# A grouped 1x1 convolution on one core: a longer head, unrolled pairs moved ahead of the loop, other store sizes at both ends, another relief for DMA engines

## The chip, the cores and the metric

One core of one Trainium2 chip runs the kernel. The metric is the device time in microseconds (us), median of several runs; before the change it was 478.7 us (three runs, 478.02 to 479.0). The record marks all executions told of here as fast; where one execution of a kernel took longer than another, it is called long, not slow. "PE" is the matmul engine, "ACT" the scalar engine, "DVE" the vector engine, "POOL" and "SP" two engines that here mostly issue transfers. The page counts 16 DMA engines for the core; they move the data between HBM and the on-chip memory, SBUF (here 201.57 MB in 10674 packets).

## The reference, cut to what matters

```python
def reference(x, w):              # x: 1 x 512 x 512 x 192, bf16;  w: 1 x 1 x 4 x 48 x 48
    ...
    # k = 1: each pixel's 4 groups of 48 channels are multiplied by 4 small matrices
    out = out + jnp.einsum('bhwgc,gcd->bhwgd', xg[:, i:i+H, j:j+W, :, :], w[i, j])
    return out.reshape(B, H, W, C)
```

262144 pixels of 192 bf16 channels are read and as many written: 100.7 MB each way. There is little arithmetic per byte.

## The kernel before

Each of the 128 partitions (rows) of SBUF takes a run of pixels; a "column" is one pixel per row, 384 bytes of it. Loads fill a ring of 240 columns, stores leave from a second ring of 280. Four columns are a "group", eight a "pair". For a pair, PE transposes 12 blocks and multiplies 12 blocks, DVE copies the transposed data, ACT copies ("casts") the result into the store ring. SP issues loads, ACT stores.

Two things are unusual. First, most of PE's program is a loop of 30 pairs, run 8 times, with unrolled pairs ahead of it and after it. Second, twice in the kernel 48 columns are moved as "120-row pieces": 8 of the 128 rows get no data there, and the rest is cut into blocks. In the trace one DMA engine gets no packet of these pieces (engine 4 below, idle for 1.9 us). In one of the two pieces some further rows move fewer columns (`UNEVEN`, "the relief").

```python
BIG = 80
SLOTS = 3
RCOLS = SLOTS * BIG                 # load ring, columns
OGRID = (72, 140, 212, 280)         # where stores end in the store ring
HEAD = (8, 24, 48)                  # first loads, columns
LATE_COLS = 240                     # the last 240 columns are stored in parts of 40,
LATE_PART = 40                      # the very last in 24, 20, 16 and 8
LAST_PARTS = (24, 20, 16, 8)
FULL = (("sync", 0, 128, 128, 0),)  # queue, first row, rows, outer size, columns less
PARTIAL = (
    ("sync", 0, 16, 4, 0), ("sync", 32, 16, 4, 0),
    ("pool", 52, 44, 11, 0), ("pool", 20, 12, 3, 0), ("pool", 96, 32, 8, 0),
)
UNEVEN = (("sync", 0, 16, 4, 16), *PARTIAL[1:])
FRONT = ((6, ((48, PARTIAL), (32, FULL))), (11, ((48, UNEVEN), (32, FULL))))
# ... (planning of fields, pieces, stores and of the loop cut)

            # PE
            for first, body, rounds in LOOPS:           # before: [(9, 30, 8)]
                for pair in range(pair, first):
                    step(pair)                          # unrolled: 9 pairs
                with pe.Fori(0, rounds):
                    for pair in range(first, first + body):
                        step(pair)
                pair = first + rounds * body
            for pair in range(pair, NP):
                step(pair)                              # unrolled: 8 pairs
# ...
            # ACT
            for g in range(NG):
                act.wait_ge(mm_done, g + 1)
                while todo and stores[todo[0]].g1 <= g - 1:
                    issue(todo.pop(0))                  # a store, when its last group is cast
                if over[g] is not None:
                    landed(over[g])                     # wait: the store last held in these columns
                v = 2 * g
                act.copy(out_columns(g).rearrange("p (u c) -> p u c", u=2),
                         o_ps[:, v % NOB:v % NOB + 2, 0:UC]).then_inc(...)
```

Of the kernel before, what the change touches and what calls it, by code (L numbers as in the profile page):

```python
# [1 line left out]

# [22 lines left out]
BIG = 80  # L25
SLOTS = 3
RCOLS = SLOTS * BIG
OGRID = (72, 140, 212, 280)
OCOLS = OGRID[-1]
HEAD = (8, 24, 48)  # L30
LATE_COLS = 240
LATE_PART = 40
LAST_PARTS = (24, 20, 16, 8)
NXP = 4
NXS = 3
NOB = 4
# [4 lines left out]
PARTIAL = (  # L41
    ("sync", 0, 16, 4, 0), ("sync", 32, 16, 4, 0),
    ("pool", 52, 44, 11, 0), ("pool", 20, 12, 3, 0), ("pool", 96, 32, 8, 0),
)
UNEVEN = (("sync", 0, 16, 4, 16), *PARTIAL[1:])
FRONT = ((6, ((48, PARTIAL), (32, FULL))), (11, ((48, UNEVEN), (32, FULL))))

FILL_ROWS = 5
FILL_BEFORE = (2, 3)


class Field:


    def __init__(self, cols, blocks, g0, pix):
        self.cols, self.g0, self.g1 = cols, g0, g0 + cols // 4
        self.full = blocks is FULL
        self.blocks = []
        for (queue, r0, rows, outer, less) in blocks:
            self.blocks.append((queue, r0, rows, outer, pix, cols - less))  # L60
            pix += rows * (cols - less)
        self.pix_end = pix
        assert cols % 4 == 0


class Piece:

    def __init__(self, i, field, c0, size):
        self.i, self.field = i, field
        self.c0, self.c1, self.size = c0, c0 + size, size  # L70
        self.g0, self.g1 = field.g0 + self.c0 // 4, field.g0 + self.c1 // 4
        self.at = 4 * self.g0 % RCOLS
        self.full, self.blocks = field.full, field.blocks
        assert size % 4 == 0 and self.at + size <= RCOLS

# [8 lines left out]
def plan_fields(npix):  # L84

    parts, head = [], sum(HEAD)
    for slots, special in FRONT:
        parts += [(head + BIG * slots, FULL), *special]
        head = 0
    cols = npix - sum((n - b[4]) * b[2] for n, blocks in parts for b in blocks)  # L90
    if cols < 128 * BIG:
        parts, cols = [], npix
    assert cols % 512 == 0
    fields, g, pix = [], 0, 0
    for n, blocks in [*parts, (cols // 128, FULL)]:
        fields.append(Field(n, blocks, g, pix))
        g, pix = fields[-1].g1, fields[-1].pix_end
    assert pix == npix
    return fields


def plan_pieces(fields):
    pieces = []
    for f in fields:
        first = [f.cols]
        if f.full:
            first = list(HEAD) if not f.g0 and sum(HEAD) <= f.cols else []
        c = 0
        while c < f.cols:
            n = first.pop(0) if first else min(BIG, f.cols - c)  # L110
            pieces.append(Piece(len(pieces), f, c, n))
            c += n
    return pieces


def plan_stores(fields):
    total = 4 * fields[-1].g1
    stores, at = [], 0
    for f in fields:
        c = 0  # L120
        if not f.full and at + f.cols > OCOLS:
            at = 0
        ends = []
        if f is fields[-1] and f.cols > LATE_COLS:
            ends = [f.cols - sum(LAST_PARTS[i:]) for i in range(len(LAST_PARTS))]
        while c < f.cols:
            if f.full:
                end = min([g for g in OGRID if g > at + 24] or [OCOLS]) - at + c
                if f.cols < BIG:
                    end = min(OCOLS - at + c, f.cols)  # L130
                if ends and c >= f.cols - LATE_COLS:
                    end = min(OCOLS - at, LATE_PART) + c
                end = min([end, f.cols] + [e for e in ends if e > c])
            else:
                end = f.cols
            stores.append(Store(f, c, end, at))
            c, at = end, (at + end - c) % OCOLS
    return stores


class Unit:


    def __init__(self, pieces):
        self.pieces, self.g0, self.g1 = pieces, pieces[0].g0, pieces[-1].g1
        self.slot = pieces[0].at // BIG
        self.regular = pieces[0].at % BIG == 0 and 4 * (self.g1 - self.g0) == BIG


def plan_units(pieces):  # L150
    units, rest = [], list(pieces)
    while rest:
        n = 1
        if rest[0].g0 and rest[0].at % BIG == 0:
            while n < len(rest) and rest[n].at % BIG:
                n += 1
        units.append(Unit(rest[:n]))
        rest = rest[n:]
    return units
# [19 lines left out]
def bass_standalone__grouped__vision_kernel(nc, x, w, out):  # L179
# [5 lines left out]
    fields = plan_fields(npix)  # L185
    pieces = plan_pieces(fields)
    stores = plan_stores(fields)
    units = plan_units(pieces)
    unit_of = {g: u for u in units for g in range(u.g0, u.g1)}
    store_of = {g: s for s in stores for g in range(s.g0, s.g1)}  # L190
# [12 lines left out]
    def transfers(ap, tile, part, queues):  # L203
        f, c0, c1, at = part.field, part.c0, part.c1, part.at
        for n, (queue, r0, rows, outer, pix, cols) in enumerate(f.blocks):
            if queue not in queues:
                continue
            px = ap[pix:pix + rows * cols, :]
            if f.full:
                view = px.rearrange("(p i) n -> p (i n)", p=rows)[:, c0 * C:c1 * C]  # L210
            else:
                assert (c0, c1) == (0, f.cols)
                view = px.rearrange("(c a i) n -> a c (i n)", a=outer, c=rows // outer)
            yield n, view, tile[r0:r0 + rows, at * C:(at + (c1 - c0 if f.full else cols)) * C]
# [12 lines left out]
    with ExitStack() as es:  # L227
# [25 lines left out]
        fill_sem = [sem(f"fill{k}") for k in range(4 * len(mixed))]  # L253

        def columns(g):
            at = 4 * g % RCOLS
            return ring[:, at * C:(at + 4) * C]

        def out_columns(g):
# [9 lines left out]
        def _(gp):  # L269
# [12 lines left out]
            def filler():  # L282
                k = len(used)
                src = xf[0:2 * FILL_ROWS, 0:4].rearrange("(t p) n -> p t n", t=2)
                dst = fill[:, 8 * k:8 * k + 8].rearrange("p (t n) -> p t n", t=2)
                gp.dma_start(dst, src).then_inc(fill_sem[k], 16)  # L286
                used.append(k)

            for nth, u in enumerate(mixed):
                part = [p for p in u.pieces if not p.full]  # L290
                for p in part:
                    gp.wait_ge(t_done, freed(p))
                    for n, dram, sbuf in transfers(xf, ring, p, ("pool",)):
                        if n in FILL_BEFORE:
                            filler()
# [6 lines left out]
                for i, s in enumerate(stores):  # L302
                    if any(s.field is p.field for p in part):
                        for n, dram, sbuf in transfers(of, oring, s, ("pool",)):
                            if n in FILL_BEFORE:
                                filler()
# [16 lines left out]
        def _(pe):  # L323
# [12 lines left out]
            def transposes(pair):  # L336
                todo = []
                for g in groups(pair):
                    u = unit_of[g]
                    if g % 2 and pair:  # L340
                        pe.wait_ge(e_done[(pair - 1) % NTOK], 1)
                    if g == u.g0:
                        for key in unit_keys[u]:
                            pe.wait_ge(ld_sem[key], 16)
                        todo += unit_keys[u] if u.regular else []
                    xg = columns(g)
                    for ul in range(2):
                        for tc in range(3):
                            j = ul * 3 + tc
                            last = pe.transpose(xT_ps[:, g % NXP, j * 128:(j + 1) * 128],  # L350
                                                xg[:, j * 128:(j + 1) * 128], ident[:])
                            if todo and 0 < j < 5:
                                last.then_inc(ld_sem[todo.pop(0)], -16)
                assert not todo
                last.then_inc(t_done, 1)
# [125 lines left out]
```

## Time and profile before

| what | value | where it stands |
|---|---|---|
| time | 478.7 us (three runs) | times |
| bytes moved, mean rate | 201.6 MB, 423 GB/s | page, DMA line |
| PE, ACT busy | 431.7, 388.3 us of 476.1 | page, part 1 |
| last cast ends | 467.7 us | timeline |
| last store lands | 475.6 us | landing times in the trace |

The page of the kernel before: PE's busy time and share, and of the 40 slices of the span the busy tenths of PE and DMA, and the GB/s in each slice:

```profile
PE 431.7 (91%) x6178; PEld 389.5 (82%) x6178; DVE 246.8 (52%) x258; ACT 388.3 (82%) x515; POOL 12.5 (3%) x28
...
PE   5999999999598999999998896999978979999991
...
DMA  8999999999999999999999999999999999999996
GB/s 330 439 394 431 429 423 432 432 430 428 435 431 429 434 421 435 435 429 433 439 431 428 428 436 433 424 427 434 433 434 424 439 422 425 433 432 432 420 424 287
```

DMA is at nine tenths or more in all slices but the first and the last, PE has dips. This reads as transfers that set the pace and compute that waits for them. The chain of waits says the same: its longest links (start, length, what) are four transfers.

```profile
89.78 39.13 DMA ring<-in_x_dram
...
239.06 49.44 DMA out_dram<-oring
...
306.59 44.66 DMA out_dram<-oring
...
385.64 44.65 DMA out_dram<-oring
```

The waits view (who waits for whom: total us, times, longest) shows what this costs ACT and PE:

```profile
ACT oring L446 <- DMA out_dram<-oring: 15.2, 7, 3.4
PEld xT_ps L350 <- POOLq L300: 5.1, 1, 5.1
```

The second line is the wait for a load of a 120-row piece (POOL collects its blocks). Then the windows view, two early stretches and the last two (window, length, busy us and count of PE, PEld, DVE, ACT and POOL, granted clock, DMA share, GB/s; a packet is counted whole in the window where it starts, so a share can pass 1):

```profile
12.00:24.00 12.00, 11.88 (x177) 10.72 (x175) 7.35 (x8) 10.90 (x15) 0.00 (x0) 1.00 1.04 448
24.00:36.00 12.00, 11.71 (x179) 10.75 (x177) 6.85 (x8) 10.87 (x15) 0.00 (x0) 1.00 0.96 380
...
456.00:468.00 12.00, 9.93 (x138) 8.44 (x136) 4.84 (x6) 10.45 (x14) 0.00 (x0) 1.00 0.99 413
468.00:480.00 12.00, 0.00 (x0) 0.00 (x0) 0.00 (x0) 0.00 (x0) 0.00 (x0) 0.61 0.38 155
```

The rate falls to 380 GB/s at 24 to 36 us although the engines are busy 0.96 of it. At the end, compute is over (no engine busy after 468 us) while DMA still works. The last line of the timeline (start, length) puts the last store's issue at 467.76 us, some 8 us ahead of its landing:

```profile
466.93 0.80 ACT L446 CAST oring<-o_ps 128x768 bf16<-128x768 f32 x1 [0.21 <-issue]
467.76 0.34 ACTq L427 DMA_DIRECT2D out_dram<-oring  x1
```

**Reading the packets one by one.** A DMA record in the trace has a start, a duration, a size and a queue, but no engine. It can be rebuilt: on a busy engine the next packet's record starts 4 ns before the last one's ends. Followed back from the 16 last packets, with each engine's order of sizes known from the plan, the records from 40 us on fall into 16 rows; 99.6% of 9593 steps have that 4 ns to within 6 ns. An engine's share of the 120-row pieces then tells its group. The kernel cuts these pieces into two blocks of 16 rows (SP loads and ACT stores them) and blocks of 44, 12 and 32 rows that POOL issues. (It also issues tiny filler transfers of 5 rows ahead of the 44-row and the 12-row block.) Of the 16 rebuilt rows four have packets of the SP and ACT blocks, one has none of the pieces, and eleven have POOL blocks, three of them from the 12-row block and eight from the 32-row block. They are called engines 0 to 3 (SP and ACT blocks), 4 (no block), 5 to 7 (12-row block) and 8 to 15 (32-row block) here. The numbers are names of groups: no record gives an engine's number.

When each engine's last packet ends, kernel before (us):

```
engines 0-3    470.3 470.5 472.8 473.4
engine  4      470.3                       (idle 1.9 us; no other group over 0.3 us)
engines 5-7    472.0 472.6 472.7
engines 8-15   471.7 472.1 473.0 473.5 473.7 473.7 473.9 475.2     mean of all 472.6, last 475.2
```

The trace also has packets of 16 KB that load no data; the page lists them under a queue of kind "instruction":

```profile
q8 instruction: 9, 0.15, 0.1%
```

They are called fetches here. Seven start between 17.3 and 71.3 us and two at 457.7 and 467.4 us; each takes 0.88 to 1.04 us of one DMA engine. The author puts them down to PE, because they pause while PE runs its loop: none starts between 71.3 and 457.7 us. The engine that ends at 475.2 us served the one at 467.4.

Engine 4 is the one that the 120-row pieces spare: its 30720-byte loads take 1154 ns in the median and its 27648-byte stores 1098 ns; each of the others needs 1138 and 1025 ns.

### The profile page before, as it was taken

Reading aid. Unit: us, or ns where it says so; the run is one execution under the profiler, and the core shown is the slowest. Engines: PE = TensorE matmul, PEld = TensorE weight load, DVE = VectorE, ACT = ScalarE, POOL = GpSimd, SP = SyncE. Lnnn points to the kernel's source line nnn. Section 1 sums busy time; section 2 is a strip of 40 time slices with the busy share of each in tenths; the row PEclk is TensorE's granted clock in tenths of the full one; section 3 lists DMA queues with packets and bytes.
Section 4 is the critical chain, followed back from the end, with each engine's and each line's share of the span. In section 5 each row is a group of like instructions: output and inputs, shape, how many; then the busy total and the mean of one; then the engine's idle time right before and its main releaser. Section 6 shows DMA issues by size and latency. Waiting matters only on the chain.

```text
span 476.1 us, 13580 instructions
## 1 busy us (share of the span) xinstructions
PE 431.7 (91%) x6178; PEld 389.5 (82%) x6178; DVE 246.8 (52%) x258; ACT 388.3 (82%) x515; POOL 12.5 (3%) x28
## 2 busy tenths in 40 slices
PE   5999999999598999999998896999978979999991
PEld 5888888888597988888987796898877977988880
DVE  2655555555255555555554453555535545555550
ACT  2898899988477898999987785899968968988882
POOL 1000000200002000000000000200002000000000
PEclk9999999999889999999999997999989989999996
DMA  8999999999999999999999999999999999999996
GB/s 330 439 394 431 429 423 432 432 430 428 435 431 429 434 421 435 435 429 433 439 431 428 428 436 433 424 427 434 433 434 424 439 422 425 433 432 432 420 424 287
DMA packets 10674, 201.57 MB, mean 423 GB/s; under 512 B 2112, under 2 KB 2112, under 8 KB 2752
## 3 DMA queue, kind: packets, MB, share of 16 engines
q1 hardware_dynamic: 4320, 97.44, 48.0%
q10 hardware_dynamic: 5120, 97.42, 47.8%
q0 software_dynamic: 1216, 6.49, 3.3%
q8 instruction: 9, 0.15, 0.1%
q14 instruction: 9, 0.07, 0.0%
HBM read 100.68 MB, written 100.66 MB: 423 GB/s over the span
## 4 chain that ended last, share of the span: by engine, by line
PE 48%; DMA 39%; ACT 8%; ACTq 1%; issue 1%; another core or an unknown queue 1%; SPq 0%; POOLq 0%
DMA out_dram<-oring 29%; PE o_ps L370 28%; PE xT_ps L350 20%; DMA ring<-in_x_dram 9%; ACT oring L446 8%; ACTq L427 1%; SPq L320 0%; SPq L313 0%; ACTq L420 0%; POOLq L300 0%; POOLq L299 0%; ACTq L429 0%
## 5 line engine op out<-in xcount | busy, mean ns | idle before, releaser
L446 ACT CAST oring<-o_ps 128x768 bf16<-128x768 f32 x514 | 387.0, 801 | 78.6 <-PE o_ps L370 56.7
L409 DVE COPY xT_sb<-xT_ps 128x1536 bf16<-128x1536 bf16 x257 | 246.1, 958 | 214.8 <-PE xT_ps L350 214.8
L370 PE MATMUL o_ps<-wt,xT_sb 128*128 128x144 bf16 (+1 forms) x3084 | 289.5, 236 | 24.2 <-ACT oring L446 18.5
L370 PEld LDWEIGHTS o_ps<-wt,xT_sb 128*128 128x128 bf16 x3084 | 212.6, 99 | 63.2 <-ACT oring L446 54.3
L350 PE MATMUL xT_ps<-ident,ring 128*128 128x128 bf16 x3084 | 222.4, 222 | 7.9 <-POOLq L300 4.9
L350 PEld LDWEIGHTS xT_ps<-ident,ring 128*128 128x128 bf16 x3084 | 190.1, 100 | 10.9 <-POOLq L300 5.1
L286 POOL DMA_DIRECT2D fill<-in_x_dram x8 | 4.6, 573 | 350.5 <-PE xT_ps L350 233.1
L296 POOL DMA_DIRECT2D ring<-in_x_dram x6 | 3.3, 559 | 0.0
L307 POOL DMA_DIRECT2D out_dram<-oring x6 | 3.3, 556 | 0.0
L332 PE MATMUL o_ps<-w_sb,esel 48*128 48x48 bf16 x10 | 0.6, 210 | 2.7 <-DMA w_sb<-in_w_dram 2.7
L332 PEld LDWEIGHTS o_ps<-w_sb,esel 48*128 48x128 bf16 x10 | 0.5, 113 | 2.7 <-POOL esel L273 2.7
L402 DVE CAST wt<-o_ps 128x480 bf16<-128x480 f32 x1 | 0.7, 658 | 3.3 <-PE o_ps L332 3.3
L446 ACT ACT_TABLE_LOAD x1 | 1.3, 1283 | 0.8 <-PEq L466 0.8
L273 POOL TENSOR_SCALAR_AFFINE_SELECT esel<-esel 48x272 bf16<-48x272 bf16 x1 | 0.4, 402 | 0.0
L270 POOL MEMSET esel<- 48x272 bf16 x1 | 0.3, 317 | 0.3 <-POOLq L466 0.3
L277 POOL TENSOR_SCALAR_AFFINE_SELECT ident<-ident 128x128 bf16<-128x128 bf16 x1 | 0.3, 282 | 0.0
L271 POOL MEMSET ident<- 128x128 bf16 x1 | 0.2, 198 | 0.0
L466 POOL MEMSET const-float32-0.0<- 128x1 f32 x1 | 0.1, 98 | 0.3 <-issue 0.3
L466 POOL MEMSET const-bfloat16-1.0<- 128x1 bf16 x1 | 0.1, 101 | 0.0
L466 POOL MEMSET const-uint8-127<- 128x1 uint8 x1 | 0.1, 101 | 0.0
L466 POOL MEMSET const-float32-1.0<- 128x1 f32 x1 | 0.1, 98 | 0.0
## 6 DMA issues: line engine op xcount, KB each, us to landing
ring<-in_x_dram SPq DMA_DIRECT2D x22, 3840.0 KB, 26.0
out_dram<-oring ACTq DMA_DIRECT2D x11, 3456.0 KB, 39.5
out_dram<-oring ACTq DMA_DIRECT2D x10, 3264.0 KB, 39.6
out_dram<-oring ACTq DMA_DIRECT2D x3, 1920.0 KB, 21.1
out_dram<-oring ACTq DMA_DIRECT2D x1, 3840.0 KB, 44.7
ring<-in_x_dram SPq DMA_DIRECT2D x2, 1536.0 KB, 32.8
out_dram<-oring ACTq DMA_DIRECT2D x2, 1536.0 KB, 40.8
out_dram<-oring ACTq DMA_DIRECT2D x1, 2880.0 KB, 37.2
```

The source lines that it names most:

```text
L273: gp.affine_select(out=esel[:], in_=esel[:], pattern=[[-1, ECOLS]], compare_op=AluOpType.is_equal, fill=0.0, base=ESHIFT, channel_multipli ...
L286: gp.dma_start(dst, src).then_inc(fill_sem[k], 16)
L296: gp.dma_start(sbuf, dram).then_inc(ld_sem[ld_key[p.i, n]], 16)
L307: gp.dma_start(dram, sbuf).then_inc(st_sem[i][n], 16)
L332: last = pe.matmul(o_ps[:, NOB - 1, col:col + CG], lhsT=esel[:, s0:s0 + 128], rhs=w_sb[:, g, :], start=True, stop=True, skip_group_check=True)
L350: last = pe.transpose(xT_ps[:, g % NXP, j * 128:(j + 1) * 128], xg[:, j * 128:(j + 1) * 128], ident[:])
L370: last = pe.matmul(o_ps[:, v % NOB, c0_:c1_], lhsT=xs[:, j * 128:(j + 1) * 128], rhs=wt[:, WOFF[tc]:WOFF[tc] + (c1_ - c0_)], start=(tc == ...
L402: dve.tensor_copy(wt[:], o_ps[:, NOB - 1, 0:WCOLS]).then_inc(wc_sem, 1)
L409: dve.tensor_copy(xT_sb[pair % NXS][:, 0:n * 2 * UC].rearrange("p (g c) -> p g c", g=n), xT_ps[:, b0:b0 + n, 0:2 * UC]).then_inc(e_done[pa ...
L427: act.dma_start(dram, sbuf).then_inc(st_sem[i][n], 16)
L446: act.copy(out_columns(g).rearrange("p (u c) -> p u c", u=2), o_ps[:, v % NOB:v % NOB + 2, 0:UC]).then_inc(fa_done[g % (2 * NTOK)] if g < ...
L466: nc = _bacc.Bacc("TRN2", target_bir_lowering=False, num_devices=1)
```

## The change

The intent, read from the diff: begin to store after 8 columns instead of 72; move all unrolled pairs but one ahead of the loop (16 before, 1 after; it was 9 and 8), for which the head grows from 80 to 136 columns; end with fewer, larger stores; and in the second 120-row piece take 8 columns off rows 0 to 15 (was 16) and 4 off rows 96 to 127 (was 0). The number of stores, 37, and of bytes stays.

```diff
--- before.py
+++ after.py
@@ -1,4 +1,5 @@
 from contextlib import ExitStack
+from itertools import accumulate
 
 import concourse.bass as bass
 from concourse import mybir
@@ -27,10 +28,11 @@
 RCOLS = SLOTS * BIG
 OGRID = (72, 140, 212, 280)
 OCOLS = OGRID[-1]
-HEAD = (8, 24, 48)
-LATE_COLS = 240
-LATE_PART = 40
-LAST_PARTS = (24, 20, 16, 8)
+HEAD = (8, 24, 48, 56)
+FIRST_STORES = (8, 24, 40)
+LATE_COLS = 96
+LATE_PART = 60
+LAST_PARTS = (28, 16, 8)
 NXP = 4
 NXS = 3
 NOB = 4
@@ -42,11 +44,16 @@
     ("sync", 0, 16, 4, 0), ("sync", 32, 16, 4, 0),
     ("pool", 52, 44, 11, 0), ("pool", 20, 12, 3, 0), ("pool", 96, 32, 8, 0),
 )
-UNEVEN = (("sync", 0, 16, 4, 16), *PARTIAL[1:])
+UNEVEN = (("sync", 0, 16, 4, 8), *PARTIAL[1:4], ("pool", 96, 32, 8, 4))
 FRONT = ((6, ((48, PARTIAL), (32, FULL))), (11, ((48, UNEVEN), (32, FULL))))
 
 FILL_ROWS = 5
 FILL_BEFORE = (2, 3)
+
+
+def ring_at(g):
+
+    return (4 * g - sum(HEAD)) % RCOLS
 
 
 class Field:
@@ -69,7 +76,7 @@
         self.i, self.field = i, field
         self.c0, self.c1, self.size = c0, c0 + size, size
         self.g0, self.g1 = field.g0 + self.c0 // 4, field.g0 + self.c1 // 4
-        self.at = 4 * self.g0 % RCOLS
+        self.at = ring_at(self.g0)
         self.full, self.blocks = field.full, field.blocks
         assert size % 4 == 0 and self.at + size <= RCOLS
 
@@ -120,15 +127,15 @@
         c = 0
         if not f.full and at + f.cols > OCOLS:
             at = 0
-        ends = []
+        ends = list(accumulate(FIRST_STORES)) if not f.g0 and f.cols > OCOLS else []
         if f is fields[-1] and f.cols > LATE_COLS:
-            ends = [f.cols - sum(LAST_PARTS[i:]) for i in range(len(LAST_PARTS))]
+            ends += [f.cols - sum(LAST_PARTS[i:]) for i in range(len(LAST_PARTS))]
         while c < f.cols:
             if f.full:
                 end = min([g for g in OGRID if g > at + 24] or [OCOLS]) - at + c
                 if f.cols < BIG:
                     end = min(OCOLS - at + c, f.cols)
-                if ends and c >= f.cols - LATE_COLS:
+                if f is fields[-1] and f.cols > LATE_COLS and c >= f.cols - LATE_COLS:
                     end = min(OCOLS - at, LATE_PART) + c
                 end = min([end, f.cols] + [e for e in ends if e > c])
             else:
@@ -144,14 +151,14 @@
     def __init__(self, pieces):
         self.pieces, self.g0, self.g1 = pieces, pieces[0].g0, pieces[-1].g1
         self.slot = pieces[0].at // BIG
-        self.regular = pieces[0].at % BIG == 0 and 4 * (self.g1 - self.g0) == BIG
+        self.regular = self.g0 > 0 and pieces[0].at % BIG == 0 and 4 * (self.g1 - self.g0) == BIG
 
 
 def plan_units(pieces):
     units, rest = [], list(pieces)
     while rest:
         n = 1
-        if rest[0].g0 and rest[0].at % BIG == 0:
+        if 4 * rest[0].g0 >= sum(HEAD) and rest[0].at % BIG == 0:
             while n < len(rest) and rest[n].at % BIG:
                 n += 1
         units.append(Unit(rest[:n]))
@@ -253,7 +260,7 @@
         fill_sem = [sem(f"fill{k}") for k in range(4 * len(mixed))]
 
         def columns(g):
-            at = 4 * g % RCOLS
+            at = ring_at(g)
             return ring[:, at * C:(at + 4) * C]
 
         def out_columns(g):
```

## The prediction

> **What bounds it now.** The 16 DMA engines. The page's slices show DMA busy 0.9 or more in all but the first and last slice, at 420 to 439 GB/s. PE is busy 91% and ACT 82%, but the windows view has PE at only 9.5 to 10.5 of 12 us around 144, 252 to 288, 348 and 384 us. There it waits for data: the chain of waits holds one load of 39.1 us (at 89.8) and stores of 49.4, 44.7 and 44.7 us. The last cast ends at 467.7 us; DMA still moves 410 GB/s at 468 to 470 us, and the last store lands at 475.6 us. So the end is DMA backlog, not compute.
>
> The trace's packet records allow more: a packet of 30720 bytes takes 1138 ns (27 GB/s per engine, 432 for 16[...]), and on one engine the next packet starts when the last one ends. Following packets backwards from the end gives 16 unbroken rows. Fifteen have no idle time to speak of after 40 us. They end at 470.3 to 475.2 us, mean 472.7. Identified by their share of the 120-row pieces (16-row blocks on engines 0 to 3, nothing on engine 4[...]; the rows agree): engines 0 to 3 end at 470.3, 470.6, 472.8, 473.4; engine 4 at 470.3; 5 to 7 at 472.0, 472.6, 472.7; 8 to 15 at 471.7 to 473.9, and one at 475.2. That last one also serves an instruction fetch (16 KB, 0.96 us) at 467.4 us.
>
> **What the change does.**
> - Relief: rows 0 to 15 lose 8 columns instead of 16, so engines 0 to 3 gain 8 x 4 rows x 384 B, loaded and stored: 24.6 KB, 0.91 us (estimate from the packet rate). Rows 96 to 127 lose 4 columns, so engines 8 to 15 lose 0.46 us. The slowest goes to about 474.8; engines 0 to 3 reach at most 474.3. Gain at the end: 0.4 to 0.5 us.
> - Tail: PE unrolls 16 pairs before its loop and one after, instead of 9 and 8. The fetch now at 457.7 us moves to about 80 us. An engine that never idles loses the same 0.96 us either way. The fetch at 467.4 [...]probably stays. Gain: about 0, or up to 0.9 if it vanishes.
> - Early stores: the first store now starts at 25.8 us; it will start near 12 us. DMA is busy already, so bytes are only reordered. Load packets take 0.97 us per engine longer than usual at 27 to 31 us, just when stores begin; I expect that to move rather than vanish. Gain 0.2.
> - Last stores: 28, 16, 8 columns, same count overall (37). Behind a 4 us backlog their size does not show.
> - Compute: same matmuls and casts; off the critical path.
>
> Sum: about -0.8 us, nearly all from balance, not from less work. Time: 477.9 us, range 476.2 to 479.3. Faster by over 2%: 0.01; within 2%: 0.98; slower: 0.01.
>
> **What would show it.** Last landings spread under 5 us instead of 5.0, and the last at about 474.8 us; the slow load packets near 12 to 16 us instead of 27 to 31; a fetch near 80 us and none at 457; casts still ending before 470 us; DMA busy unchanged in the middle.
>
> **What would make it wrong.** If early stores remove the 1 us of slow packets: 1 us faster. If the final fetch vanishes: 0.5 to 0.9 faster. If larger late stores leave engines without queued work, or the moved ring positions make the cast wait for stores longer so that compute ends after 471 us: slower by 1 to 3 us.

(Three clauses are cut, since no trace or run of this case shows them: a rate, a ground for naming the engines, and a reason for the place of the last fetch. None is a term of the sum, which came to about -0.8 us as recorded. That engines lose or gain bytes by the rows named, and that an engine loses the same 0.96 us wherever a fetch falls, are the author's estimates from the rebuilt trace: 27 GB/s for each engine, and 964 ns for the fetch at 467.4 us.)

## The result, and the profile after

The changed kernel: 478.27 us median of six runs (477.63 to 480.13), the kernel before 478.85 us in six. The ratio is 1.000 with a 95% interval of 0.9976 to 1.0024. Here and below a ratio is the mean time of one kernel's fast runs over that of the other's of the same rounds, so it is not quite the ratio of the medians. Two more comparisons on other chips gave 0.9991 (0.9958 to 1.0025) and 1.0021 (0.9994 to 1.0049). So the time is the same to about 0.2%; the predicted -0.8 us (-0.17%) is too small to be told from nothing by these times. The traces tell more.

The page after (same lines):

```profile
PE 430.8 (90%) x6178; PEld 389.4 (82%) x6178; DVE 246.9 (52%) x258; ACT 388.9 (82%) x515; POOL 12.5 (3%) x28
...
PE   4999999999988999699987999888999896999991
...
DMA  8999999999999999999999999999999999999997
GB/s 329 425 422 425 427 441 425 430 434 425 431 433 432 426 433 427 423 441 431 430 428 432 436 421 429 433 434 424 424 435 419 427 416 417 427 437 429 431 415 319
```

The third slice has risen from 394 to 422 GB/s and the last from 287 to 319. Late slices have fallen: those from 381 to 405 us (33rd and 34th) move 416 and 417 GB/s, before 422 and 425. The windows:

```profile
12.00:24.00 12.00, 11.59 (x174) 10.48 (x172) 6.92 (x8) 10.65 (x14) 0.00 (x0) 1.00 1.00 423
24.00:36.00 12.00, 11.73 (x176) 10.65 (x175) 7.05 (x8) 10.86 (x15) 0.00 (x0) 1.00 1.00 418
...
456.00:468.00 12.00, 9.57 (x134) 8.03 (x131) 4.84 (x6) 10.14 (x14) 0.00 (x0) 1.00 0.97 415
468.00:480.00 12.00, 0.00 (x0) 0.00 (x0) 0.00 (x0) 0.00 (x0) 0.00 (x0) 0.58 0.46 193
```

The dip at 24 to 36 us is gone, and the last stretch moves more because more is left to do: 193 GB/s for 12 us is 2.3 MB, before 155 and 1.9 MB. The longest links of the chain of waits are transfers again, all stores now; the 39 us load of the 120-row piece has left it:

```profile
127.61 48.64 DMA out_dram<-oring
...
210.87 47.30 DMA out_dram<-oring
...
274.93 47.57 DMA out_dram<-oring
...
354.07 48.78 DMA out_dram<-oring
```

The end of the timeline, then two waits:

```profile
466.75 0.80 ACT L453 CAST oring<-o_ps 128x768 bf16<-128x768 f32 x1 [0.28 <-issue]
467.58 0.34 ACTq L434 DMA_DIRECT2D out_dram<-oring  x1
```

```profile
ACT oring L453 <- DMA out_dram<-oring: 19.3, 8, 4.4
...
PEld xT_ps L357 <- POOLq L307: 1.5, 1, 1.5
```

Compute ends at 467.55 us, as before. PE's wait for the 120-row load is shorter, ACT's waits for stores are longer; they trade places, as they would where the transfers set the pace. The engines' ends now:

```
engines 0-3    471.3 471.4 473.3 474.1
engine  4      470.1
engines 5-7    473.3 475.4 475.6
engines 8-15   471.9 473.4 474.4 474.5 474.7 475.1 475.3 475.3     mean of all 473.7, last 475.6
```

(In this trace 5 to 7 and 8 to 15 are told apart less surely: two of the rows mix both patterns.) The last engine stands 1.9 us above the mean instead of 2.6, so the balance is better by 0.7 us. But the mean has gone up by 1.1 us. No engine moves more bytes to speak of; the same packets take longer. Let "slow time" be what the data packets of 3072 bytes or more (instruction fetches left out) take above the usual, that is the median, duration of their size, summed and divided by 16. From 12 to 36 us it is 0.47 us per engine (before 0.99), after 36 us 3.29 (before 1.70), and over the whole execution 4.45 (before 3.41): +1.04, about the rise of the mean. These are single traces: rebuilt in the same way, the repeated run of before has its mean end at 473.4 and its last at 476.4 us (slow time 3.8 us in all), the two repeated runs of the changed kernel 473.9 and 475.9 (4.7) and 474.1 and 475.6 (4.0). So the balance is better and the mean worse in every pair, and the last engine ends at about the same time. This was not in the prediction, and it became the question for the experiments.

### The profile page after: what moved, and what is told of

Its sections match the earlier page's. It is cut to its first block, busy times and chain, and to the rows that moved or that the text cites. A ratio compares the mean times of both kernels' runs of the same rounds, so it can differ in the third digit from the quotient of the medians.

```text
span 476.4 us, 13581 instructions
## 1 busy us (share of the span) xinstructions
PE 430.8 (90%) x6178; PEld 389.4 (82%) x6178; DVE 246.9 (52%) x258; ACT 388.9 (82%) x515; POOL 12.5 (3%) x28
## 2 busy tenths in 40 slices
DMA packets 10674, 201.57 MB, mean 423 GB/s; under 512 B 2112, under 2 KB 2112, under 8 KB 2624
## 4 chain that ended last, share of the span: by engine, by line
PE 46%; DMA 42%; ACT 7%; issue 1%; another core or an unknown queue 1%; ACTq 1%; SPq 0%
DMA out_dram<-oring 40%; PE o_ps L377 27%; PE xT_ps L357 19%; ACT oring L453 7%; DMA ring<-in_x_dram 1%; ACTq L434 1%; SPq L327 0%; SPq L320 0%; ACTq L427 0%
```

## The experiments

Twelve runs, each on one chip with the kernel before beside it. Theory A, on which the prediction rests: each DMA engine is always busy, and the last of them ends the kernel. Theory B: the new order of transfers makes data packets slow later. Theory C: slow packets are chance. Later: theory R, the new relief pays back what the new order costs, and theory S, the head and the early stores cancel each other's cost.

What came of all of them, in one place (one trace each; slow time in us per engine). The number of stores, worked out from the kernels, is 37 in before, relief_only, all_rows, the changed kernel and old_relief, but 39 in first_stores and first_relief, 38 in head_only and head_relief, and 34 in last_stores: of the change's parts only the relief keeps it when made alone.

| run | head, early stores, last stores, relief | ratio to before (95%) | slow 12-36 | slow after 36 | last cast | that execution's span |
|---|---|---|---|---|---|---|
| before | old, old, old, old | | 0.99 | 1.70 | 467.7 | 476.1 |
| rep_before | old, old, old, old | 0.9987 (0.9956-1.0017) | 1.15 | 2.02 | 469.7 | 477.3 |
| relief_only | old, old, old, new | 0.9992 (0.9961-1.0023) | 1.18 | 1.76 | 468.0 | 476.2 |
| last_stores | old, old, new, old | 1.0003 (0.9991-1.0015) | 1.11 | 1.84 | 468.3 | 476.1 |
| first_stores | old, new, old, old | 1.0061 (1.0047-1.0075) | 0.45 | 2.45 | 469.2 | 476.1 |
| first_relief | old, new, old, new | 1.0046 (1.0018-1.0075) | 0.41 | 3.04 | 469.7 | 478.1 |
| head_only | new, old, old, old | 1.0066 (1.0039-1.0092) | 0.82 | 3.48 | 469.4 | 477.1 |
| head_relief | new, old, old, new | 1.0050 (1.0016-1.0083) | 0.67 | 5.14 | 473.6 | 480.7 |
| old_relief | new, new, new, old | 1.0022 (0.9990-1.0054) | 0.61 | 3.82 | 472.5 | 481.0 |
| old_relief2 | new, new, new, old | 1.0041 (1.0009-1.0072) | 0.45 | 3.95 | 470.2 | 477.8 |
| after | new, new, new, new | 1.0000 (0.9976-1.0024) | 0.47 | 3.29 | 467.5 | 476.4 |
| rep_after | new, new, new, new | 0.9991 (0.9958-1.0025) | 0.50 | 3.50 | 468.8 | 476.7 |
| after3 | new, new, new, new | 1.0021 (0.9994-1.0049) | 0.51 | 2.84 | 471.3 | 476.4 |
| all_rows | see below | 1.0248 (1.0211-1.0285) | 0.94 | 5.18 | 480.6 | 486.8 |

All results were correct.

### rep_before: the kernel before again (no edit)

> The kernel before, unchanged, to see how much one execution differs from the next. Theory A (the end is the last of 16 always busy DMA engines; each engine's time is its bytes at 27 GB/s plus fetches): engine ends within 0.5 us of the first trace, last near 475.2 us, time within 1 us of 478.7. Theory C (the slow data packets that the changed kernel shows after 264 us are chance, not the change): this run may show 1 to 2 us per engine of slow packets somewhere too, where its first trace had 3.5 us per engine... in all (0.22 us x 16).

(The last clause is garbled: the first trace had 3.4 us of slow time per engine in all.) Slow time came out alike, 1.15 and 2.02 us; the last engine ended at 476.4 us, 1.2 later than in the first trace, so theory A's forecast of 0.5 us was missed. Single executions of one kernel on this chip went from 477.0 to 480.6 us, so differences under 1 us are not to be read from the times of a few runs.

### rep_after: the changed kernel again (no edit)

> The changed kernel again. Theory B (the change's new order of stores and loads makes packets of engines 5 to 15 slow after 264 us): the same 1.3 us per engine of slow packets, at the same times (276, 344, 362, 382 us), mean engine end 473.6 again. Theory C (chance): the slow packets appear at other times or not at all, and without them the last engine ends near 474.5 us.

Slow time 0.50 and 3.50 us: the amounts of the first trace. The places are not quite the same: bursts of several slow packets lie near 314, 419 and 428 us here, and near 344, 362 and 383 us the first time. So the amount belongs to the kernel (against C) and the moment does not (against the letter of B).

### relief_only

```diff
-UNEVEN = (("sync", 0, 16, 4, 16), *PARTIAL[1:])
+UNEVEN = (("sync", 0, 16, 4, 8), *PARTIAL[1:4], ("pool", 96, 32, 8, 4))
```

> The kernel before with the new relief alone. Theory A: engines 0 to 3 end 0.9 us later than in the repeated run of before, engines 8 to 15 0.46 us earlier, 5 to 7 the same; time -0.5 us (0.999). Theory B: no slow packets, since order is that of before.

```
engines 0-3    471.0 471.2 474.0 474.4      before: 470.3 470.5 472.8 473.4
engine  4      470.6                                470.3
engines 5-7    471.8 472.9 472.9                    472.0 472.6 472.7
engines 8-15   472.4 472.6 472.9 473.0 473.1 473.3 473.7 475.3     mean 473.3, before 473.4
```

Engines 0 to 3 end 0.7, 0.7, 1.2 and 1.0 us later, 0.9 in the mean, the predicted size (the repeated run of before could not be rebuilt back to its 120-row pieces, so the first trace serves as the base). For 8 to 15 the 0.46 us do not show: their mean moved by 0.1 us. Two traces of the unchanged kernel differ by 0.8 us in the mean end of all engines (472.6 and 473.4), so the +0.9 us fits the prediction but is not shown by one trace. The time is the same within the interval.

### old_relief and old_relief2: the changed kernel with the old relief

```diff
-UNEVEN = (("sync", 0, 16, 4, 8), *PARTIAL[1:4], ("pool", 96, 32, 8, 4))
+UNEVEN = (("sync", 0, 16, 4, 16), *PARTIAL[1:])
```

> The changed kernel with the old relief (head, tail and stores changed only). Theory A: as the repeated changed kernel, but engines 0 to 3 0.9 us earlier and 8 to 15 0.46 us later; time +0.5 us against it. Theory B: slow packets after 264 us again, since they come with the order. Theory C: no tie.

> The changed kernel with the old relief, again, beside the changed kernel itself on one chip. The first time the means of six runs were 480.1 us here and 478.2 us with the new relief. Theory R (the new order makes engines 5 to 15 late, and the new relief pays that back): this is 1.5 to 2.5 us slower than the changed kernel. Theory S (the head and the early stores cancel each other's cost, the relief is worth its 0.5 us only): 0 to 0.8 us slower.

Both have slow time of the new order, 3.8 and 4.0 us after 36 us, so it does not come from the relief. On the two chips this kernel's ratio to before was 0.0031 and 0.0020 above that of the changed kernel beside it: 1.5 and 1.0 us in favour of the new relief, more than the predicted half microsecond. Each of the ratios carries about 0.003 either way, so neither difference is clear of noise by itself. The second run was to decide: its 1.0 us lies between what S expects (0 to 0.8) and what R expects (1.5 to 2.5), and decides nothing. The profiled execution of old_relief was a long one of 482.8 us; one engine ended 3.7 us after the next, and the others had run out of work (twelve ends between 475.0 and 475.2 us).

### first_stores: early stores alone

```diff
-        ends = []
+        ends = list(accumulate((8, 24, 40))) if not f.g0 and f.cols > OCOLS else []
```

(The edit is shown as against before. It was made in the changed kernel, by which the load ring was rotated by 80 columns besides; no size or order changes by that, and last_stores below has the same rotation and no loss.)

> The kernel before with only the first store of 72 columns split into 8, 24 and 40 (load ring rotated by 80 columns, which changes no size). So far, time of data packets above the shortest of their size, per engine: between 12 and 36 us 1.0 to 1.2 us in three runs with the old order and 0.5 to 0.6 in three with the new; after 36 us 1.7 to 2.0 old, 3.3 to 3.8 new. If the early stores cause both: about 0.5 and 3.5 here. If they cause only the first: about 0.5 and 1.8, mean engine end 0.5 us earlier than before.

Slow time from 12 to 36 us fell to 0.45 us: the early stores do cause that part. After 36 us it is 2.45 us, between the two orders. And the time rose by 0.6%, 1.0047 to 1.0075, clear of noise on a chip where before stayed between 477.3 and 478.6 us. The profiled execution was the fastest of the six (478.0 us; the five timed ones took 479.7 to 481.5), so its trace does not show what the slower ones lost.

### last_stores: larger late stores alone

```diff
-LATE_COLS = 240
-LATE_PART = 40
-LAST_PARTS = (24, 20, 16, 8)
+LATE_COLS = 96
+LATE_PART = 60
+LAST_PARTS = (28, 16, 8)
```

> The kernel before with only the last 240 columns stored in fewer, larger pieces. If the large late stores caused the slow packets after 36 us: about 3.5 us per engine, most of it after 400 us; since much of it came before 400 us, the theory that it is the head expects 1.8 here. Theory A (always busy engines): time as before within 1 us, tail invisible behind the backlog.

1.0003, 0.9991 to 1.0015; slow time as before. The tail's store sizes do not show in the time, as predicted.

### head_only: the longer head, and with it the loop without tail

```diff
-HEAD = (8, 24, 48)
+HEAD = (8, 24, 48, 56)
```

(With the changed kernel's ring and loop bookkeeping, and old first stores, last stores and relief. The longer head also rotates the load ring by 136 columns, moves the 120-row pieces 14 groups later and cuts the stores around them otherwise; the run can't tell these apart.)

> The kernel before with only the head of 136 columns (loop shifted by 7 pairs, last 120-row pieces 14 groups later, no unrolled tail). If the head causes the slow packets after 36 us: about 3.5 us per engine, and 1.1 between 12 and 36 us; mean engine end +1.5 us, near 474.3. Fetches by the matmul engine at 80 and 88 us and none after 450 us, so no single engine of 8 to 15 ends over 1 us after the others. Time +0.5 to +1.5 us.

Slow time 3.48 us after 36 us, as the theory of the head expects, and 0.82 before. PE's instruction fetches came at 79.9 and 89.0 us, none after 450 us. No engine stands far behind the others: rebuilt, the last two end at 475.8 and 476.3 us. Time +0.66%, 3 us: more than the slow time accounts for, and than the 0.5 to 1.5 us expected.

### first_relief and head_relief: each of the two with the new relief

> The kernel before with the early stores and the new relief. With the old relief it was 1.0061. Theory R: 1.000 to 1.003. Theory S: 1.005 to 1.006, as the head is missing that would cancel the cost.

> The kernel before with the head of 136 columns and the new relief. With the old relief it was 1.0066. Theory R: 1.001 to 1.003. Theory S: 1.005 to 1.006.

1.0046 and 1.0050, close to the 1.0061 and 1.0066 with the old relief. This speaks against theory R: the new relief hardly heals either alone, though the intervals (from 1.0018 and from 1.0016) still reach what R expects. Early stores alone cost about 0.5%, the head alone about 0.5%; both together cost next to nothing with the new relief (1.0000, 0.9991, 1.0021) and 0.2 to 0.4% with the old. That is as theory S has it, but S is not shown: all kernels with both had the new last stores too, which take stores away (34 instead of 37 alone) where the head and the early stores add some, so these may have a part in it, and no run has both with the old last stores.

The trace of head_relief caught a long execution, and shows what happens in one. Windows and the end of the timeline:

```profile
456.00:468.00 12.00, 11.59 (x169) 10.21 (x167) 6.70 (x7) 10.35 (x15) 0.00 (x0) 1.00 0.97 413
468.00:480.00 12.00, 3.95 (x53) 3.09 (x49) 1.91 (x2) 5.06 (x7) 0.00 (x0) 0.74 0.66 276
```

```profile
472.81 0.80 ACT L453 CAST oring<-o_ps 128x768 bf16<-128x768 f32 x1 [0.22 <-issue]
473.64 0.34 ACTq L434 DMA_DIRECT2D out_dram<-oring  x1
```

Here compute ended 6 us later than before the change. Eleven of 16 engines end between 476.1 and 476.4 us, right behind the last store: they had no backlog left. Three laggards end at 478.3 to 479.9 us.

### after3: the changed kernel, third time (no edit)

> The changed kernel, third time. Both theories: 0.998 to 1.002 of before. Slow packets after 36 us: 3.2 to 3.8 us per engine again if they belong to the order.

1.0021, barely outside the range expected; slow time 2.84 us after 36 us, less than expected but above all runs of the old order. In this trace compute ended late, as the end of the timeline shows:

```profile
470.46 0.80 ACT L453 CAST oring<-o_ps 128x768 bf16<-128x768 f32 x1 [0.28 <-issue]
471.29 0.34 ACTq L434 DMA_DIRECT2D out_dram<-oring  x1
```

Rebuilt, twelve engines end within 0.2 us, at 473.8 to 474.0 us, having just run out of work when the last store came; the last ends at 475.6 us, and the time is no longer than others (478.16 us).

### all_rows: the eight rows moved too, meant for engines 0 to 3

```diff
 PARTIAL = (
     ("sync", 0, 16, 4, 0), ("sync", 32, 16, 4, 0),
+    ("sync", 16, 4, 4, 0), ("sync", 48, 4, 4, 0),
     ("pool", 52, 44, 11, 0), ("pool", 20, 12, 3, 0), ("pool", 96, 32, 8, 0),
 )
-UNEVEN = (("sync", 0, 16, 4, 16), *PARTIAL[1:])
+UNEVEN = PARTIAL
```

(`FILL_BEFORE`, which counts blocks, goes from (2, 3) to (4, 5) with the two new ones. That the new blocks run on engines 0 to 3, as the two 16-row blocks do in the rebuilt trace of before, is the author's estimate: the engines of this run are not told here.)

> The kernel before, where the 8 rows left out of the 120-row pieces are given to engines 0 to 3 as well (two more transfers of 4 rows each way), no column left out, 8 columns less in all. Each of engines 0 to 3 moves 0.147 MB more for those rows, 0.049 less for the shorter whole, 0.049 more for the column relief that is gone: +5.5 us; all others -1.8 us. Theory A: the last engine is now of 0 to 3, near 473.4 + 5.5 = 478.9 us, and time +3.5 us (1.0075). If the end were set by the sum of bytes or by compute: -1.8 us or 0.

It took 488.4 us: +11.8 us by the ratio (0.0248 of 477.6), over three times the expected 3.5. The sign speaks for theory A (fewer bytes in all, yet slower), the size against its simple form. The waits and windows show why:

```profile
ACT oring L447 <- DMA out_dram<-oring: 21.1, 6, 12.1
PEld xT_ps L351 <- POOLq L301: 12.2, 1, 12.2
```

```profile
456.00:468.00 12.00, 11.70 (x173) 10.35 (x170) 6.71 (x7) 10.34 (x15) 0.00 (x0) 1.00 0.75 314
468.00:480.00 12.00, 10.64 (x145) 8.94 (x144) 5.74 (x6) 10.73 (x15) 0.00 (x0) 1.00 0.69 284
```

Compute waited 12 us at once for the late blocks, once for a load (before 5.1) and once for a store (before 3.4 at most). It never made that up: the last cast ended at 480.6 us, and from 456 to 480 us the DMA engines were busy only 0.75 and 0.69 of the time. So late blocks in the middle of this kernel cost more, 11.8 us, than the 5.5 us of work that the estimate adds to engines 0 to 3: compute had only a small reserve (it ended 8 us ahead of the last landing in the trace of before).

## Why the prediction was right or wrong

The total was right: no change beyond noise, inside the range. That says little of the sum behind it: the range (476.2 to 479.3 us) also holds no change at all, and the interval of the ratio is about 1.2 us either way. Of the prediction's own signs, two failed: the last landings spread over 5.5 us (470.1 to 475.6) instead of under 5, and the last came at 475.6 us instead of 474.8. So it was in part luck that the total fitted: a term that the prediction lacked took back about what it had counted on. Step by step:

1. **"The 16 DMA engines bound it" - right.** Both traces have the engines busy to the end, compute ends 8 us ahead of the last landing, and the last stores' sizes alone make no difference (1.0003). The packet of 30720 bytes takes 1138 ns in both, 27.0 GB/s; 16 of them make 432 GB/s, and the mean over the span was 423 in both.
2. **"Engines 0 to 3 +0.91 us" - fits; "8 to 15 -0.46 us" - not seen.** relief_only showed +0.9 and -0.1, in one trace. In the changed order the relief came out at 1.0 to 1.5 us, neither clear of noise alone, in the old order at nothing measurable.
3. **"The fetch at 457.7 us moves to about 80" - right. "The fetch at 467.4 probably stays" - wrong.** It moved too: the nine 16 KB fetches of PE now come between 17 and 88 us. **"An engine loses the same 0.96 us either way" - doubtful.** Of the six traces of the old head with nine fetches, five have the last engine be the one that served the late fetch, three of them 1.3 to 2.0 us behind the next, one 0.9 and one less than 0.1. But with early fetches only, the last engine can lag as well: by 0.1 to 1.0 us in six traces, and by 3.7 in old_relief. No run moved the fetch alone, so this is argued from the traces, not shown by an experiment.
4. **"Slow packets move rather than vanish; gain 0.2" - mis-sized, and the missing term.** The 0.97 us at 27 to 31 us became 0.5 us between 12 and 36 us; first_stores shows that early stores do this. What the prediction did not have: slow time after 36 us rises from 1.7-2.0 us in the four runs with the old head, old first stores and 120-row pieces to 2.8-4.0 us in the five with new head, first and last stores (whichever relief). all_rows, with the old head and stores but other pieces, has 5.2 us, so other changes to the transfers bring it too. In all, slow time is 3.4 and 3.8 us in the two traces of before and 4.0 to 4.7 in the three of the changed kernel: 0.2 to 1.3 us more per engine, of the size of everything gained. The largest part of the growth after 36 us is in SP's load packets: 0.5 to 0.6 us in the four old runs, 1.3 to 2.1 in the five new, while ACT's store packets go from 1.2-1.3 to 1.4-1.8. The longest single delay after 36 us in the trace of after is 0.96 us: 26112-byte packets near 345 us took 1924 ns, in the median 968.
5. **"Compute: off the critical path" - right for the shorter executions, with less reserve than thought.** At the last cast some 1.9 MB are left to store (155 GB/s for 12 us), about 4 us of work at 430 GB/s. The traced executions above 480 us (all_rows apart) had the last cast at 472.5 and 473.6 us, and most engines were then out of work. The prediction named this as a way to be wrong ("compute ends after 471 us"); head_relief, old_relief and all_rows went that way; of the changed kernel's three traces one did too (after3, last cast at 471.3 us), without a longer time.

So a gain of the expected size shows in the balance of the engines (the last 1.9 instead of 2.6 us above the mean), and it was given back by slower packets in the middle (mean end +1.1 us). This is the reading of the traces, not of an experiment: the times can't tell -0.8 us from nothing, and whether the balance came from the relief or from the moved fetches stays open. Rebuilt traces with one of the two have the last engine 2.5 us (relief_only), 2.1 (head_only) and 2.4 us (old_relief2) above the mean, against 1.5 to 2.0 in the three of the changed kernel and 2.6 and 3.0 in the two of before. What stays open: why the same packets take longer in the new order, and why the head and the early stores, each costing about 0.5% alone, cost -0.1 to 0.2% together with the new relief. No version was found that beats both kernels; relief_only and the changed kernel are level with before.

## What to carry to other kernels

Here, where the DMA engines were busy nearly all the time (nine tenths or more in all slices but the first and the last), the new order of transfers saved no bytes (201.57 MB before and after), and equal packets took longer in it (slow time 3.4 and 3.8 us per engine before, 4.0 to 4.7 after). In such a kernel, add up each engine's work and look at the last one, and check in the trace whether the same packets still take the same time. A change whose parts each cost half a per cent alone was neutral as a whole (1.0046 to 1.0066 alone, 0.9991 to 1.0021 together with the new relief), so judge parts of a tuned schedule together as well as one by one. A reserve of a few microseconds between compute and the transfers' end is worth keeping: where late blocks ate it, the loss was a few times the expected one (all_rows: 11.8 us against 3.5).
